# Seed tables of an S4D convolution: the second halves of five of eight sets made inside the attention loop

## The chip, the cores and the metric

The kernel runs on one core of a Trainium2 chip. The metric is device time in microseconds (us) of one execution. The core has five engines with an instruction queue each: TensorE (PE; its weight loads are listed as PEld), VectorE (DVE), ScalarE (ACT), GpSimd (POOL) and SyncE (SP), which issues all of this kernel's DMAs. Each engine takes its instructions in order, and waits on semaphores for the others.

## The reference

Two independent halves are computed and put side by side. Half A is a state-space convolution (S4D): a kernel K of 2048 taps for each of 448 channels is a sum over 256 complex modes, and it is convolved with the input u. Half B is attention with 16 heads of 28 channels over 2048 positions.

```python
dt = jnp.exp(log_dt)
A = -jnp.exp(log_A_real) + 1j * A_imag
C = (C_real + 1j * C_imag) * dt[:, None]
P = jnp.exp((A * dt[:, None])[:, :, None] * pos[None, None, :])
K = 2.0 * jnp.einsum("dn,dnl->dl", C, P).real
...
y = jnp.fft.irfft(Uf * Kf[None, :, :], L2)[:, :, :L]
y = y + u * D_skip[None, None, :]
...
qkv = (x @ wqkv).reshape(B, S, 3, H, Dh).transpose(2, 0, 3, 1, 4)
scores = jnp.einsum("bhqd,bhkd->bhqk", q, k) * scale
p = softmax(scores, axis=-1)
o = jnp.einsum("bhqk,bhkd->bhqd", p, v).transpose(0, 2, 1, 3).reshape(B, S, D) @ wo
return jnp.concatenate([a, b], axis=-1)
```

## The kernel before

The program has a prologue and a loop of 256 steps.

The prologue makes two things side by side. First, the projections of x to q, k and v, 48 of them, each of twelve matmuls; their results (`hl`, `vst`) are stored in DRAM. Second, the seeds. K is built in 56 blocks of 8 channels (`NB = 56`), and each block starts from a small table, its seeds: the first few powers of exp(A dt), C times such powers, and the factors for doubling. Seeds are made in eight sets (`NO = 8`) of seven blocks (`BO = 7`) by `seeds(o)`, which gives thirteen stages; set o begins four stages after set o - 1, and the 48 projections are spread over the first 37 stages (`PW = 37`). A set has a first half (load, exponent, scaling by dt, transposes on TensorE, phases, reduction, sines, sizes) which leaves the tile `tri` with cosine, sine and size of eleven powers (`LV = 11`). The second half multiplies these: `places`, `e_base`, `g_base`, `g_first`, `factors`, `g_copies` and two complex products on VectorE and GpSimd (`e3`, `e5`) fill the tiles `se` (named `qhat` in the profile, whose memory it borrows) and `sg`. `put_g` and `put_e` store them in `sd_d[o]`. Instructions of the prologue may be moved by the scheduler of the build.

At its end the prologue loads the first group's keys, q and v, and makes the row maxima of the first query unit (the max pass), 64 matmuls, each followed by a VectorE or ScalarE op.

The loop runs over 16 units (4 head groups x 4 chunks of 512 queries) of 16 key tiles each, so a group has 64 steps. Here every engine keeps the order of the program, which `ORDER` writes out for a step: four max matmuls (`m`, for the unit 16 + 3 steps ahead), four score matmuls (`s`) with an exponential on ScalarE each, the product with v (`pv`), two slots for other work (`f`), three places for VectorE (`v`), one place `k` for the kernel blocks. The other work:

- The kernel blocks of half A: `load_sd` brings a block's seeds, `e_power` (GpSimd, nine ops) and `g_powers` (VectorE) double them up to 64 and 32 powers, `k_mm` multiplies them on TensorE. A block may begin every `KP = 3.5` steps.
- The transform of u, in slots from step 3 to about 103.
- From step 192 (`12 * NK`) the spectra, and then the finish jobs, of half A, when the memory of the first keys is free; the second half of them, once the last kernel block is done.

Max matmuls, kernel blocks and all other work in the loop share three work banks of PSUM (`w_tile`). A group's keys fill the tile `khat` of 32 KB a partition; two such tiles (`k0_p`, `kq_p`) alternate between groups. `load_k` brings the next group's keys, one head at a time, at steps 17, 21, 25 and 29 of a group. The max matmuls of the next group begin at step 45 of a group.

Operands of VectorE inside the loop: `g_powers` works on `g` in SBUF and `zg` in PSUM, the maxima read PSUM, or PSUM and `rl` in SBUF.

Of the kernel before, what the change touches and what calls it, by code (L numbers as in the profile page):

```python
# [8 lines left out]
F32 = mybir.dt.float32  # L9
# [3 lines left out]
ALU = mybir.AluOpType  # L13
# [30 lines left out]
A0, A1, KW = 26, 34, (33, 35, 36)  # L44

# [45 lines left out]
def body(ctx, tc, a, out):  # L91
# [15 lines left out]
    sd_d = [dram.tile([BO, 128, SDF], F32, name=f"sd_{o}") for o in range(NO)]  # L107
    yu_d = dram.tile([128, N1, D], F32, name="yu_d")
# [102 lines left out]

    with ExitStack() as st:
# [97 lines left out]
        NH = BO * 16  # L310
        mul = lambda e, o_, x_, y_: e.tensor_tensor(o_, x_, y_, ALU.mult)

        def seeds(o):
# [5 lines left out]
            v = lambda t, k: t[:, k, :].rearrange("p (b h) -> p b h", h=16)  # L319
            vk = lambda t, k: t[:, k:k + 3, :].rearrange("p k (b h) -> p k b h", h=16)  # L320
# [8 lines left out]
            def turn():  # L329
                q["ps"] = ps = ps_n.tile([128, CQ], F32, name="pn")[:, :8 * PO].rearrange("p (a b h e) -> p a b h e", a=4, h=2, e=8)  # L330
                for i in range(4):
                    for h in range(2):
                        nc.tensor.transpose(ps[:, i, :, h, :], q["nat"][:, i, h * 128:(h + 1) * 128], ident[:PO, :PO])
                q["tr"] = s_p.tile([128, NH], F32, name="tr", bufs=2)
                act.activation(q["tr"], ps[:, 0].rearrange("p b h e -> p (b h e)"), AF.Copy)

            def phases():
                tri = t_p.tile([128, 3, LV, NH], F32, name="tri", bufs=2)
# [20 lines left out]
            def places():  # L359
                se = q_p.tile([128, HG, CQ], F32R, name="qhat", bufs=3).bitcast(F32).rearrange("p h q -> p (h q)")  # L360
                q["se"] = se = se[:, :BO * F_G].rearrange("p (b f) -> p b f", f=F_G)
                q["sg"] = sg = s_p.tile([128, BO, SDF - F_G], F32, name="sg", bufs=SGB)
                q["e8"] = se.rearrange("p b (c h e) -> p b c h e", c=2, e=8)
                q["g4"] = sg[:, :, :F_Z - F_G].rearrange("p b (c h e) -> p b c h e", c=2, e=4)
                q["zz"] = sg[:, :, F_Z - F_G:].rearrange("p b (k f h) -> p k b f h", k=6, f=3)
                pol.memset(q["e8"][:, :, 0, :, 0], 1.0)
                pol.memset(q["e8"][:, :, 1, :, 0], 0.0)

            def e_base():
                for k in range(3):  # L370
                    mul(pol, q["e8"][:, :, 0, :, 1 << k], v(q["mg"], k), v(q["r"], k))
                    mul(pol, q["e8"][:, :, 1, :, 1 << k], v(q["mg"], k), v(q["sn"], k))

            def g_base():

                q["gz"] = gz = s_p.tile([128, 2, 2, NH], F32, name="gz")
                mul(pol, q["r"][:, 6:8, :], q["mg"][:, 6:8, :], q["r"][:, 6:8, :])
                mul(pol, gz[:, :, 0], q["mg"][:, 6:8, :], q["sn"][:, 6:8, :])
                act.activation(gz[:, :, 1], gz[:, :, 0], AF.Copy, scale=-1.0)

            def g_first():

                c0 = q["ps"][:, 2:4].rearrange("p c b h e -> p c (b h e)")
                px = ps_x.tile([128, CQ], F32, name="px")
                c1, x_ = (px[:, i:i + 2 * NH].rearrange("p (c n) -> p c n", c=2) for i in (0, 2 * NH))
                g4_ = lambda e: q["sg"][:, :, :F_Z - F_G].rearrange("p b (c h e) -> p c b h e", c=2, e=4)[:, :, :, :, e]
                bh = lambda t: t.rearrange("p c (b h) -> p c b h", h=16)
                zr = lambda k: q["r"][:, 6 + k, :][:, None, :].to_broadcast([128, 2, NH])
                tt = vec.tensor_tensor
                for k, src, e, dst in ((0, c0, 1, bh(c1)), (1, c0, 2, g4_(2)), (1, c1, 3, g4_(3))):  # L390
                    tt(g4_(e), bh(src), bh(zr(k)), ALU.mult)
                    tt(x_, src[:, ::-1], q["gz"][:, k], ALU.mult)
                    tt(dst, g4_(e), bh(x_), ALU.add)
                q["c"] = c0, c1

            def g_copies():
                for c in range(2):
                    for e in range(2):
                        act.activation(q["g4"][:, :, c, :, e], q["c"][e][:, c].rearrange("p (b h) -> p b h", h=16), AF.Copy)

            def factors(i, k, p_, n_):
                zz, mg = q["zz"], q["mg"]
                mul(vec, zz[:, i:i + 3, :, 0, :], vk(mg, k), vk(q["r"], k))
                mul(vec, zz[:, i:i + 3, :, p_, :], vk(mg, k), vk(q["sn"], k))
                for k in range(i, i + 3):
                    act.activation(zz[:, k, :, n_, :], zz[:, k, :, p_, :], AF.Copy, scale=-1.0)

            def cmul(e, dst, s0, n, wr, wi, conj):

                if e is nc.vector:  # L410
                    x_ = ps_x.tile([128, CQ], F32, name="px")[:, :BO * 16 * n].rearrange("p (b h e) -> p b h e", h=16, e=n)
                else:
                    x_ = s_p.tile([128, BO, 16, 4], F32, name="x_e")[:, :, :, :n]
                br, bi = (w_[:, :, :, None].to_broadcast([128, BO, 16, n]) for w_ in (wr, wi))
                for c in range(2):
                    mul(e, dst[c], s0[c], br)
                    mul(e, x_, s0[1 - c], bi)
                    e.tensor_tensor(dst[c], dst[c], x_, ALU.add if (c == 0) == conj else ALU.subtract)

            sl = lambda t, i0, i1: [t[:, :, c, :, i0:i1] for c in range(2)]  # L420
            e8 = lambda *i: sl(q["e8"], *i)
            e3 = lambda: cmul(vec if o % 8 < E3 else pol, e8(3, 4), e8(1, 2), 1, q["e8"][:, :, 0, :, 2], q["e8"][:, :, 1, :, 2], False)
            e5 = lambda: cmul(pol, e8(5, 8), e8(1, 4), 3, q["e8"][:, :, 0, :, 4], q["e8"][:, :, 1, :, 4], False)
# [8 lines left out]
            fa, fb = lambda: factors(0, 3, 2, 1), lambda: factors(3, 8, 1, 2)  # L432
            return [[load], [exp_a] + dts(1, 2, 3), dts(0), [turn], [phases], [reduce], [sines], [sizes, g_base],
                    [places, fa, e_base], [e3, g_first], [fb, e5, g_copies], [put_g], [put_e]]
# [70 lines left out]
        n_stage = SP * (NO - 1) + len(stages[0])  # L505
# [110 lines left out]
    def load_sd(b):  # L616
        sds[b] = g_p.tile([128, SDF], F32, name="sdb", bufs=4)
        nc.sync.dma_start(sds[b], sd_d[b // BO][b % BO])
# [55 lines left out]

    def k_mm(b):
# [296 lines left out]
    def k_seed(s_):  # L972
        b = k_due[0] if k_due else NB
        if b < NB and b not in egs and done["mm"] >= b - 2 and K0 + b * KP <= s_ + (1 if b in es else 2):
# [31 lines left out]
    for s in range(NS):  # L1006
# [20 lines left out]
        if kt % 4 == 1 and u % NQ == 1 and u // NQ + 1 < G:  # L1027
            load_k(u // NQ + 1, kt // 4, k_pools[(u // NQ + 1) % 2])
# [4 lines left out]
        for op in ORDER:  # L1033
# [6 lines left out]
            elif op == "k":  # L1040
# [89 lines left out]
```

## Time and profile before

| what | value |
|---|---|
| median of 3 runs | 1301.34 us (1301.32 to 1303.18) |
| span of the profiled execution | 1301.1 us |
| mean granted TensorE clock | 0.978 |
| first score matmul of the loop | 254.0 us |
| last score matmul | 1275.7 us |
| busy: PE, DVE, ACT, POOL | 94%, 73%, 73%, 67% |
| HBM read, written | 120.73 MB, 82.18 MB |

The profile is of one execution. "Busy" is the union of an engine's instructions; matmuls are pipelined, so a busy TensorE need not be at its peak. A group of instructions is named by its engine, operation and tiles (out<-in). "A <-B" beside an idle time says that the engine sat idle until B was done. All lines of the kernel have the same line number in the profile, since a helper records every instruction; one goes by tiles. A timeline row gives start, duration, engine and instruction.

### The profile page before, as it was taken

What the parts mean: (1) busy time and instruction counts of PE and PEld (TensorE: products, weight loads), DVE (VectorE), ACT (ScalarE), POOL (GpSimd) and SP (SyncE); (2) the same over time, 40 slices, a digit from 0 to 9 for tenths busy, and PEclk for the clock granted to TensorE, in tenths of its full rate; (3) what the DMA queues carried; (4) which work ended last, traced back from release to release, by engine and by line L of the source; (5) the groups of instructions that cost most, each with busy time, mean ns of one, the idle gap of its engine ahead of it and who ended that gap; (6) DMA issues with size and microseconds to landing.
All of it is one profiled execution on the core that took longest, in us unless ns stands there. A gap on an engine that the chain in (4) does not pass through costs nothing.

```text
span 1301.1 us, 33177 instructions
## 1 busy us (share of the span) xinstructions
PE 1228.2 (94%) x12625; PEld 701.0 (54%) x12625; DVE 948.0 (73%) x2106; ACT 952.4 (73%) x2068; POOL 871.1 (67%) x736
## 2 busy tenths in 40 slices
PE   6878985899999999999999999999999999999997
PEld 5657763355555555555555555555555555544433
DVE  5887896987777887787788888888888655645111
ACT  4775763488888888888888888888887766756552
POOL 3676683298888878888869999998996212424421
PEclk9888997999999999999999999999999999999999
DMA  6677769835866555458644131733425453647656
GB/s 194 203 258 244 249 206 294 237 77 124 195 137 149 124 146 148 140 147 231 181 126 96 54 95 32 182 91 83 103 51 148 153 158 133 201 144 244 198 162 174
DMA packets 200088, 205.35 MB, mean 158 GB/s; under 512 B 95993, under 2 KB 158521, under 8 KB 197881
## 3 DMA queue, kind: packets, MB, share of 16 engines
q1 hardware_dynamic: 199928, 203.23, 56.2%
q8 instruction: 100, 1.64, 0.5%
q14 instruction: 60, 0.48, 0.1%
HBM read 120.73 MB, written 82.18 MB: 156 GB/s over the span
## 4 chain that ended last, share of the span: by engine, by line
PE 71%; DVE 10%; DMA 6%; POOL 5%; ACT 3%; issue 3%; SPq 0%; POOLq 0%; ACTq 0%; DVEq 0%
PE pm L75 40%; PE pss L75 16%; PE po L75 15%; DVE tri L75 2%; DVE mx L75 2%; POOL e L75 1%; POOL qhat L75 1%; DMA k<-hl 1%; ACT tri L75 1%; DVE qhat L75 1%; DVE sg L75 1%; DMA tri<-in_B_wqkv 1%; DVE px L75 1%; DMA khat<-k 1%; DMA ut<-in_A_u 1%
## 5 line engine op out<-in xcount | busy, mean ns | idle before, releaser
L75 ACT ACTIVATE p<-pss 128x512 f32<-128x512 f32 x1024 | 560.9, 609 | 111.6 <-PE pss L75 108.6
L75 PE MATMUL pss<-qhat,khat 128*128 128x512 f32 x1024 | 402.5, 399 | 1.5 <-ACT p L75 1.4
L75 DVE TENSOR_REDUCE mx<-pm 128x1 f32<-128x512 f32 x500 | 321.4, 684 | 109.2 <-PE pm L75 107.1
L75 PE MATMUL pm<-khat,qhat 128*128 128x512 f32 x749 | 326.3, 438 | 3.4 <-DVE mx L75 2.1
L75 POOL TENSOR_TENSOR e<-e,sdb 128x256 f32<-128x256 f32 x168 | 202.0, 1202 | 116.2 <-ACT e L75 61.2
L75 PE MATMUL po<-p,v 128*32 128x512 f32 x2048 | 269.1, 594 | 0.0
L75 POOL TENSOR_TENSOR e<-e,eu 128x256 f32<-128x256 f32 x168 | 248.4, 1478 | 13.2
L75 PEld LDWEIGHTS pm<-khat,qhat 128*128 128x128 f32 x749 | 141.0, 189 | 199.7 <-ACT p L75 47.8
L75 DVE CUSTOM_DVE_ANT_0 rl<-pm,rl 128x512 f32<-128x512 f32 x249 | 171.4, 688 | 65.2 <-ACT rl L75 61.5
L75 PEld LDWEIGHTS pss<-qhat,khat 128*128 128x128 f32 x1024 | 190.2, 188 | 45.7 <-issue 10.8
L75 POOL TENSOR_TENSOR eu<-e,sdb 128x256 f32<-128x256 f32 x168 | 202.2, 1203 | 0.0
L75 POOL TENSOR_TENSOR p<-pr,pr 64x448 f32<-64x448 f32 x64 | 73.3, 1145 | 158.5 <-PE pm L75 133.2
L75 ACT ACTIVATE rl<-pm 128x512 f32<-128x512 f32 x249 | 150.8, 606 | 20.4 <-PE pm L75 20.4
L75 DVE TENSOR_TENSOR g<-g,zg 128x128 f32<-128x128 f32 x392 | 162.1, 413 | 3.4
L75 PE MATMUL pm<-xh,khat 112*128 112x512 f32 x256 | 94.1, 451 | 23.2 <-DVE hl L75 11.1
L75 PE MATMUL pm<-kdif,qhat 128*128 128x512 f32 x249 | 100.5, 404 | 2.6 <-DMA v<-v 1.3
L75 DVE TENSOR_TENSOR zg<-g,zg 128x128 f32<-128x128 f32 x224 | 88.0, 393 | 5.0
L75 PEld LDWEIGHTS pm<-e,g 128*32 128x32 f32 x3584 | 57.2, 109 | 43.8 <-issue 16.1
L75 DVE TENSOR_TENSOR pr<-pm,ub 128x448 f32<-128x448 f32 x64 | 37.0, 619 | 56.4 <-PE pm L75 42.0
L75 PEld LDWEIGHTS pm<-xh,khat 112*128 112x128 f32 x256 | 54.2, 217 | 39.4 <-DVE hl L75 12.9
L75 PE MATMUL pm<-e,g 128*32 128x64 f32 x3584 | 73.0, 222 | 1.9 <-POOL e L75 1.9
L75 ACT ACTIVATE y<-pm 128x448 f32<-128x448 f32 x48 | 26.5, 553 | 58.2 <-PE pm L75 33.8
(134 smaller groups left out, 1470.3 us busy)
## 6 DMA issues: line engine op xcount, KB each, us to landing
sdb<-sd SPq DMA_DIRECT2D x56, 336.0 KB
khat<-k SPq DMA_DIRECT2D x64, 256.0 KB
qhat<-q SPq DMA_DIRECT2D x64, 256.0 KB
sd<-sg SPq DMA_DIRECT2D x8, 1456.0 KB
k<-hl SPq DMA_DIRECT2D x16, 512.0 KB
q<-hl SPq DMA_DIRECT2D x16, 512.0 KB
mw<-in_mw SPq DMA_DIRECT2D x16, 512.0 KB
sd<-qhat SPq DMA_DIRECT2D x8, 896.0 KB
```

The costliest lines, as they stand in the source:

```text
L75: i = f(*args, **kw)
```

## The change

Sets 0, 1 and 2 are made as before. For sets 3 to 7 (`LATE`) the prologue keeps the first half only. It then stores `tri` and a copy of C (`cp`) in a new DRAM tensor `tri_d[o]`, 15.7 KB a partition. The number of stages becomes 37.

In the loop `late_products(g)` takes the `khat` tile of the next group while that group's keys aren't yet due, and makes two sets in it in group 0, two in group 1 and one in group 2, 20 steps (`WIN`) each. One DMA at the first step of a window brings the powers and C; the ops of the second half are planned on steps 2 to 16; step 17 stores `sg` and `se` in `sd_d[o]`. `se` lies in the tile `og`, which grows to 7 KB. `planned(s, kind)` issues the DMAs at the start of a step, and the engines' ops after the `k` place of a step. The next group's keys are loaded at steps 40, 44, 48 and 52 of a group (`KL = 40`) in place of 17 to 29. Kernel blocks that begin in a window are 4 steps apart (`KW0`) in place of 3.5.

The products themselves are the same functions for early and late sets (`products`), in lists of single operations; in a late set C and the intermediate results `c1` and `x` lie in the `khat` tile in SBUF, where an early set has them in PSUM (`pn`, `px`).

```diff
+LATE, WIN, KW0, KL = ((3, 4), (5, 6), (7,)), 20, 4, 40
...
+    tri_d = [dram.tile([128, 3 * LV * BO * 16 + 2 * BO * 16], F32, name=f"tri_{o}") for o in range(NO)]
...
+    def products(q, temps, x_v, x_p, e_v=None):
...
+        ops["e"] = [lambda k=k, c=c: mul(pol, q["e8"][:, :, c, :, 1 << k], v("mg", k), v(("r", "sn")[c], k))
+                    for k in range(3) for c in range(2)]
...
+        for n, i, k, p_, n_ in (("fa", 0, 3, 2, 1), ("fb", 3, 8, 1, 2)):
+            ops[n] = [lambda i=i, k=k: mul(vec, q["zz"][:, i:i + 3, :, 0, :], vk("mg", k), vk("r", k)),
+                      lambda i=i, k=k, p_=p_: mul(vec, q["zz"][:, i:i + 3, :, p_, :], vk("mg", k), vk("sn", k))]
...
+        def first(k, src, e, last):
+            zr = lambda: q["r"][:, 6 + k, :][:, None, :].to_broadcast([128, 2, NH])
+            g4 = lambda e=e: q["g4"][:, :, :, :, e]
+            return [lambda: vec.tensor_tensor(g4(), bh(q[src]), bh(zr()), ALU.mult),
+                    lambda: vec.tensor_tensor(q["x"], q[src][:, ::-1], q["gz"][:, k], ALU.mult),
+                    lambda: vec.tensor_tensor(bh(q["c1"]) if last is None else g4(last), g4(), bh(q["x"]), ALU.add)]
...
+        ops["e3"] = cmul(vec, x_v, 3, 1, 1, 2)
+        ops["e5"] = cmul(pol, x_p, 5, 1, 3, 4)
...
+            def keep_c():
+                c = s_p.tile([128, 2, NH], F32, name="cp", bufs=2)
+                act.activation(c, q["c0"], AF.Copy)
+                nc.sync.dma_start(tri_d[o][:, 3 * LV * NH:], c.rearrange("p c n -> p (c n)"))
...
+            put_tri = lambda: nc.sync.dma_start(tri_d[o][:, :3 * LV * NH], q["tri"].rearrange("p t k h -> p (t k h)"))
...
-            return [[load], [exp_a] + dts(1, 2, 3), dts(0), [turn], [phases], [reduce], [sines], [sizes, g_base],
-                    [places, fa, e_base], [e3, g_first], [fb, e5, g_copies], [put_g], [put_e]]
+            begin = [[load], [exp_a] + dts(1, 2, 3), dts(0)]
+            if o in sum(LATE, ()):
+                return begin + [[turn, keep_c], [phases], [reduce], [sines], [sizes], [put_tri]]
+            p_ = products(q, temps, x_v, x_p)
+            return begin + [[turn], [phases], [reduce], [sines], [sizes] + p_["g"] + p_["gz"],
+                            [room] + p_["ones"] + p_["fa"] + p_["fan"] + p_["e"], p_["e3"] + [sums] + p_["c"],
+                            p_["fb"] + p_["fbn"] + p_["e5"] + p_["cc"], [put_g], [put_e]]
...
-        n_stage = SP * (NO - 1) + len(stages[0])
+        n_stage = max(SP * o + len(st_) for o, st_ in enumerate(stages))
...
+    def late_products(g):
...
+        def room():
+            x["t"] = k_pools[(g + 1) % 2].tile([128, HG, L], F32R, name="khat").bitcast(F32).rearrange("p h l -> p (h l)")
...
+            def load():
+                t, c = part(3 * LV * NH), part(2 * NH)
+                nc.sync.dma_start(x["t"][:, :at[0]], tri_d[o])
...
+                se = kq_p.tile([128, BO * F_G], F32, name="og").rearrange("p (b f) -> p b f", f=F_G)
...
+            def put():
+                nc.sync.dma_start(sd_d[o][:, :, F_G:].rearrange("b p f -> p b f"), q["sg"])
+                nc.sync.dma_start(sd_d[o][:, :, :F_G].rearrange("b p f -> p b f"), q["se"])
+                put_at[o] = True
...
+            plan[s0].append(("d", load))
+            at_ = {"v": (p_["fa"] + p_["fb"] + p_["e3"] + p_["c"], (2, 2, 3, 4, 5, 6, 6, 7, 8, 9, 10, 10, 11, 12, 13, 14, 14, 15, 16)),
+                   "p": (p_["ones"] + p_["e"][:4] + p_["g"] + p_["e"][4:] + p_["e5"], (2, 2, 3, 3, 4, 4, 5, 6, 7, 8, 10, 11, 12, 13, 14, 15)),
+                   "a": (p_["fan"] + p_["gz"] + p_["fbn"] + p_["cc"], (4, 5, 6, 7, 7, 8, 9, 10, 11, 12, 13))}
...
+            plan[s0 + WIN - 3].append(("d", put))
+
+        plan[g * NQ * NK].append(("d", room))
+        for i, o in enumerate(LATE[g]):
+            one(o, g * NQ * NK + WIN * i)
...
+    slow = [s for g, o in enumerate(LATE) for s in range(g * NQ * NK, g * NQ * NK + WIN * len(o))]
+    k_at = [K0]
+    while len(k_at) <= NB:
+        k_at.append(k_at[-1] + (KW0 if int(k_at[-1]) in slow else KP))
...
-        og_u[u] = og = kq_p.tile([128, G - 1, CQ], F32, name="og")
+        og_u[u] = og = kq_p.tile([128, BO * F_G], F32, name="og")[:, :(G - 1) * CQ].rearrange("p (g q) -> p g q", q=CQ)
...
-        if not (k_due and K0 + k_due[0] * KP <= s_ and k_due[0] in egs and not powers["e"] and not powers["g"]):
+        if not (k_due and k_at[k_due[0]] <= s_ and k_due[0] in egs and not powers["e"] and not powers["g"]):
...
-        if kt % 4 == 1 and u % NQ == 1 and u // NQ + 1 < G:
-            load_k(u // NQ + 1, kt // 4, k_pools[(u // NQ + 1) % 2])
+        n = s % (NQ * NK) - KL
+        if n >= 0 and n % 4 == 0 and n < 16 and u // NQ + 1 < G:
+            load_k(u // NQ + 1, n // 4, k_pools[(u // NQ + 1) % 2])
+        planned(s, "d")
...
+                for kind in "vpa":
+                    planned(s, kind)
```

More of the change, by code (lines that the diff above doesn't have):

```diff
@@ L335, in turn @@
                 act.activation(q["tr"], ps[:, 0].rearrange("p b h e -> p (b h e)"), AF.Copy)
+                q["c0"] = ps[:, 2:4].rearrange("p c b h e -> p c (b h e)")
+            def keep_c():
+                c = s_p.tile([128, 2, NH], F32, name="cp", bufs=2)
+                act.activation(c, q["c0"], AF.Copy)
+                nc.sync.dma_start(tri_d[o][:, 3 * LV * NH:], c.rearrange("p c n -> p (c n)"))
             def phases():
-                tri = t_p.tile([128, 3, LV, NH], F32, name="tri", bufs=2)
+                q["tri"] = tri = t_p.tile([128, 3, LV, NH], F32, name="tri", bufs=2)
                 q["r"], q["sn"], q["mg"] = r, sn, mg = tri[:, 0], tri[:, 1], tri[:, 2]
@@ L357, in sizes @@
                 act.activation(q["mg"], q["mg"], AF.Exp)
-            def places():
+            def room():
                 se = q_p.tile([128, HG, CQ], F32R, name="qhat", bufs=3).bitcast(F32).rearrange("p h q -> p (h q)")
[L361 to L379, printed above, removed]
@@ L381, in g_first @@
-            def g_first():
-                c0 = q["ps"][:, 2:4].rearrange("p c b h e -> p c (b h e)")
-                px = ps_x.tile([128, CQ], F32, name="px")
[L385 to L423, printed above, removed]
+                places(q, se[:, :BO * F_G].rearrange("p (b f) -> p b f", f=F_G),
+                       s_p.tile([128, BO, SDF - F_G], F32, name="sg", bufs=SGB))
@@ new lines, in temps, with sums @@
+            def temps():
+                q["gz"] = s_p.tile([128, 2, 2, NH], F32, name="gz")
+            def sums():
+                px = ps_x.tile([128, CQ], F32, name="px")
+                q["c1"], q["x"] = (px[:, i:i + 2 * NH].rearrange("p (c n) -> p c n", c=2) for i in (0, 2 * NH))
+            x_v = lambda n: ps_x.tile([128, CQ], F32, name="px")[:, :BO * 16 * n].rearrange("p (b h e) -> p b h e", h=16, e=n)
+            x_p = lambda n: s_p.tile([128, BO, 16, 4], F32, name="x_e")[:, :, :, :n]
@@ L616, in load_sd @@
     def load_sd(b):
+        assert b // BO not in sum(LATE, ()) or put_at[b // BO]
         sds[b] = g_p.tile([128, SDF], F32, name="sdb", bufs=4)
@@ L675, in k_mm, with planned @@
+    for g in range(len(LATE)):
+        late_products(g)
+    slow = [s for g, o in enumerate(LATE) for s in range(g * NQ * NK, g * NQ * NK + WIN * len(o))]
+    k_at = [K0]
+    while len(k_at) <= NB:
+        k_at.append(k_at[-1] + (KW0 if int(k_at[-1]) in slow else KP))
+    def planned(s_, kind):
+        for k, f in plan[s_]:
+            if k == kind:
+                f()
     def k_mm(b):
@@ L973, in k_seed @@
         b = k_due[0] if k_due else NB
-        if b < NB and b not in egs and done["mm"] >= b - 2 and K0 + b * KP <= s_ + (1 if b in es else 2):
+        if b < NB and b not in egs and done["mm"] >= b - 2 and k_at[b] <= s_ + (1 if b in es else 2):
             k_seeds(b)
     def k_begin(s_):
-        if not (k_due and K0 + k_due[0] * KP <= s_ and k_due[0] in egs and not powers["e"] and not powers["g"]):
+        if not (k_due and k_at[k_due[0]] <= s_ and k_due[0] in egs and not powers["e"] and not powers["g"]):
             return
```

60 lines of the change are left out of this document (55 added, 5 removed).

## The prediction

> **What bounds the kernel now.** I read the page first: the share of each engine in 40 slices of 32.5 us, and the chain of waits.
>
> ```profile
> span 1301.1 us, 33177 instructions
> ...
> PE   6878985899999999999999999999999999999997
> ...
> DVE  5887896987777887787788888888888655645111
> ACT  4775763488888888888888888888887766756552
> POOL 3676683298888878888869999998996212424421
> PEclk9888997999999999999999999999999999999999
> DMA  6677769835866555458644131733425453647656
> ...
> PE 71%; DVE 10%; DMA 6%; POOL 5%; ACT 3%; issue 3%; SPq 0%; POOLq 0%; ACTq 0%; DVEq 0%
> ```
>
> There are two regimes. In the first eight slices (the prologue) TensorE has gaps and its granted clock is 0.8 to 0.9, with no engine full. From slice nine on (the loop) TensorE is full, and the chain is 71% TensorE; the others run at eight or nine tenths, GpSimd highest. Next come stretches of my choice: busy us and instruction count of PE, PEld, DVE, ACT and POOL, then clock, DMA share and GB/s. Two rows for the score matmuls alone (PE, PEld, ACT) follow.
>
> ```profile
> 0.00:100.00 100.00, 75.32 (x313) 58.49 (x314) 75.65 (x139) 68.37 (x134) 58.40 (x74) 0.90 0.68 221
> 100.00:212.00 112.00, 89.69 (x394) 72.59 (x392) 89.46 (x152) 70.73 (x143) 76.54 (x85) 0.90 0.74 241
> 212.00:254.00 42.00, 32.27 (x78) 15.78 (x79) 34.82 (x78) 11.86 (x21) 0.81 (x2) 0.86 0.94 264
> 254.00:650.00 396.00, 394.43 (x4626) 215.39 (x4628) 311.53 (x738) 331.36 (x764) 331.23 (x260) 1.00 0.61 150
> 700.00:950.00 250.00, 249.16 (x3048) 142.74 (x3044) 218.35 (x522) 212.11 (x481) 234.72 (x186) 1.00 0.39 93
> ...
> 300.00:650.00 350.00, 137.57 (x348) 65.45 (x348) 190.32 (x347) 1.00 0.63 157
> 700.00:950.00 250.00, 110.79 (x280) 52.66 (x280) 153.14 (x281) 1.00 0.39 93
> ```
>
> Four score matmuls make a step, so a step takes 350 / 87 = 4.02 us while the transform of u also runs (steps 3 to about 103) and 250 / 70 = 3.57 us after it. VectorE is busy 79% and 87% there, GpSimd 84% and 94%. An op added to either in the loop meets an in-order queue with 0.84 / 0.66 us free in a u step and 0.45 / 0.22 us in a later one.
>
> **What leaves the prologue.** Per seed set the second half is 19 VectorE ops, 11 ScalarE ops and 16 GpSimd ops. All eight sets together, by tile (sg: DVE, ACT; gz: DVE, ACT, POOL; qhat: PE, PEld, DVE, POOL), and one GpSimd row more:
>
> ```profile
> 0.00:212.00 212.00, 45.64 (x80) 20.21 (x80) 0.90 0.71 232
> ...
> 0.00:212.00 212.00, 9.54 (x24) 3.11 (x8) 6.74 (x8) 0.90 0.71 232
> ...
> 0.00:212.00 212.00, 0.00 (x0) 0.00 (x0) 23.53 (x48) 86.76 (x112) 0.90 0.71 232
> ...
> L75 POOL TENSOR_TENSOR tri<-tri 128x224 f32<-128x224 f32 x8 | 7.3, 912 | 9.1 <-ACT tri L75 9.0
> ```
>
> VectorE: 78.7 / 8 = 9.8 us a set; GpSimd: 100.8 / 8 = 12.6; ScalarE: 23.3 / 8 = 2.9. Five sets take 49, 63 and 15 us away, nearly all from 100 us on, against one ScalarE copy (about 0.4 us, by its like in the sg tile) and one more put a set. Here is the prologue's part of the chain of waits, its sum by line and the pieces before the max pass:
>
> ```profile
> by line: DVE tri L75 10.1%; PE pm L75 9.7%; POOL qhat L75 6.5%; DMA k<-hl 5.9%; issue 5.6%; ACT tri L75 4.9%; DVE qhat L75 4.7%; DVE sg L75 4.6%; DMA tri<-in_B_wqkv 4.0%; DVE px L75 3.9%; DMA khat<-k 3.7%; POOL tri L75 3.3%; DVE mx L75 3.1%
> ...
> 201.61 6.66 DMA q<-hl
> 208.33 12.53 DMA k<-hl
> 220.88 10.06 DMA khat<-k
> 230.95 7.58 DMA v<-v
> ...
> sd<-sg SPq DMA_DIRECT2D x8, 1456.0 KB
> ...
> sd<-qhat SPq DMA_DIRECT2D x8, 896.0 KB
> ```
>
> Upper bound: the pieces of second halves (POOL qhat, DVE qhat, sg, px: 19.7% of the first 270 us, 53 us) leave for five of eight sets, 33 us. Lower bound: the stretch 201 to 238 waits on DMAs alone, and only set 7's put (2.35 MB at the 264 GB/s of 212 to 254) leaves it: 9 us. Between them: from 100 to 212 TensorE is idle 22 us; with VectorE down from 89 to about 40 us and GpSimd to about 14, ScalarE (58) and DMA remain. DMA carries 0.74 x 112 + 0.94 x 42 = 122 us of work in 154; each late set stores 2.0 MB of powers and C in place of 2.35, some 7 us less in all. I take half to two thirds of TensorE's idle time and most of the tail, 20 us; DMA would then be 86% busy, so more is unlikely. **Prologue: -20 (-33 to -9).**
>
> **What arrives in the loop.** The same 46 ops a set, spread over 20 steps; windows lie at steps 0 to 40 and 64 to 104 (u steps) and 128 to 148 (later ones). One thing changes besides the place: the c operands lay in PSUM (pn, px) and now lie in SBUF, so all 19 VectorE ops read two SBUF tensors, while today's VectorE ops in the loop read at most one. The seed rows give min/median/max ns, then two rows of the timeline:
>
> ```profile
> L75 DVE TENSOR_TENSOR sg<-tri x32: 490/510/1171, 39.1 to 196.7; 128x336 f32<-128x336 f32 x32
> L75 DVE TENSOR_TENSOR sg<-pn,tri x16: 549/566/585, 51.9 to 206.9; 128x224 f32<-128x224 f32 x16
> ...
> L75 DVE TENSOR_TENSOR qhat<-qhat x16: 356/516/2353, 45.9 to 200.5; 128x112 f32<-128x112 f32 x16
> ...
> L75 POOL TENSOR_TENSOR qhat<-qhat x16: 1016/1024/3532, 48.6 to 203.5; 128x336 f32<-128x336 f32 x16
> ...
> 160.70 2.25 POOL L75 TENSOR_TENSOR tri<-tr,pw 128x1232 f32<-128x1232 f32 x1 [0.46 <-ACT tr L75]
> 160.90 2.35 DVE L75 TENSOR_TENSOR qhat<-qhat 128x112 f32<-128x112 f32 x1
> ```
>
> The op with one input in PSUM (sg<-pn,tri) never varies. Those with two in SBUF reach twice to six times their minimum, and the last two rows show why: VectorE's 0.36 us op lasts until GpSimd's 2.25 us op is over. GpSimd's own op was held as well, up to 3.5 times its length. GpSimd and VectorE in the loop:
>
> ```profile
> L75 POOL TENSOR_TENSOR e<-e,sdb 128x256 f32<-128x256 f32 x168 | 202.0, 1202 | 116.2 <-ACT e L75 61.2
> L75 POOL TENSOR_TENSOR e<-e,eu 128x256 f32<-128x256 f32 x168 | 248.4, 1478 | 13.2
> L75 POOL TENSOR_TENSOR eu<-e,sdb 128x256 f32<-128x256 f32 x168 | 202.2, 1203 | 0.0
> L75 DVE TENSOR_TENSOR g<-g,zg 128x128 f32<-128x128 f32 x392 | 162.1, 413 | 3.4
> L75 DVE TENSOR_TENSOR zg<-g,zg 128x128 f32<-128x128 f32 x224 | 88.0, 393 | 5.0
> ...
> L75 POOL TENSOR_TENSOR eu<-e,sdb x168: 617/1062/1922, 253.8 to 990.3; 128x256 f32<-128x256 f32 x56, 128x512 f32<-128x512 f32 x56, 128x1024 f32<-128x1024 f32 x56
> L75 POOL TENSOR_TENSOR e<-e,eu x168: 732/1303/2405, 254.5 to 992.3; 128x256 f32<-128x256 f32 x56, 128x512 f32<-128x512 f32 x56, 128x1024 f32<-128x1024 f32 x56
> ```
>
> A block of the kernel transform costs GpSimd 652.6 / 56 = 11.65 us and VectorE 250.1 / 56 = 4.47. From the three sizes, an op that comes at a random moment of GpSimd's busy time finds 0.79 us left (sum of squares over twice the sum), times 0.84 busy: 0.66 us, the upper price of a wait. Lower price: the excess that such ops have in the prologue, 23.53 / 48 = 0.49 us a piece in the qhat tile beside a minimum of 0.36, 0.13 us. I take 0.5, nearer the upper, since GpSimd is fuller here than there. A set then costs VectorE 8.5 us (9.8 less that excess on its ten two-input ops) plus 19 x 0.5 = 18 us, 0.91 us a step, and GpSimd 11 us (12.6 less what held it) plus about 7 in which VectorE's 8.5 us hold it, 0.92 a step. Blocks come every 4 steps in place of 3.5, which gives back 0.16 (VectorE) and 0.42 (GpSimd) a step. Sums a u step: VectorE 3.16 - 0.16 + 0.91 = 3.91, GpSimd 3.36 - 0.42 + 0.92 = 3.86, both beside 4.02: some 97%. TensorE stands behind VectorE through three work banks in PSUM, so I put 0.2 us of stall on each of 80 steps, 16 us (2 without the waits, 32 with 0.66). In the later window VectorE needs 3.91 and GpSimd about 3.9 beside 3.57: 0.4 us over for 20 steps, 8 us, and 4 for unevenness: 12 (0 to 18).
>
> A rule of the Trainium skill speaks against this change: SBUF — State Buffer, section "Who interferes with whom", says that a VectorE instruction with two SBUF inputs and a GpSimd one that reads SBUF exclude each other, the second to start blocking fully. The seed rows agree (0.36 us became 2.35). If every op met it at random, the upper price would hold.
>
> **The other edits.** *Loads:* a set's 2.0 MB come in one DMA issued at its first step and are used two steps later, 8.0 or 7.1 us; at 264 GB/s it takes 7.6. VectorE and GpSimd wait in order, and behind them the max reductions that free TensorE's banks: 4 us over five loads (0 to 15). *Keys* of the next group load 23 steps later, five steps (20 us) before their first max matmul, behind the set's puts in SP's queue; 1 MB a head every four steps: nothing, but a late put would stop TensorE directly. SP has 15 more issues in the loop, none long. ScalarE gains 11 short ops a set, 0.15 us a step beside some 0.65 free. *Blocks* end 12.5 steps later (25 spacings of 4); TensorE's work in them only moves. Behind the last score matmul three finish jobs stand as built, not two; the row for that stretch:
>
> ```profile
> 1275.00:1301.00 26.00, 19.74 (x270) 8.03 (x266) 3.96 (x10) 4.79 (x9) 4.18 (x2) 0.96 0.54 146
> ```
>
> Twelve finish tasks and four projections in place of eight and four, at some 2 us, partly overlapped and taken from the loop: +2 (0 to 7).
>
> Sum against the profiled 1301.1 (the median of the runs, 1301.34, is the same within what follows): 1301.1 - 20 + 16 + 12 + 4 + 2 = **1315**.
>
> **The rivals.** *Faster:* the waits fall into the 0.8 us a step in which VectorE is free anyway (it waits for TensorE then), so the loop pays 4, the loads 2, the end 2, and the prologue gives 22: 1287. For it: blocks at 4 steps hand GpSimd 0.42 us a step; against: the later window has no such room. *The prologue hardly shrinks:* the first halves stay (DVE tri is the longest line of its chain) and the DMA tail gives 9: 1301 - 9 + 34 = 1326. *A convoy:* ScalarE's sign copies wait for GpSimd's products planned one step earlier; a GpSimd late by more than 4 us stops ScalarE, and with it every exponential. It decides once GpSimd passes 100% in u steps (a wait of about 0.66): the loop's upper bounds of 32 and 18, and 15 for the loads, give 1301 - 20 + 50 + 15 = 1346. *Even:* gain and price cancel within 0.2% (2.6 us, about what a measurement here can tell from none).
>
> **Chances.** Forecast 0.39, prologue 0.12, convoy 0.10: slower 0.61. Faster 0.33, even 0.06. The forecast's own range is 1304 to 1326; 8 in 10 reach from the faster rival's better half to below the convoy: 1280 to 1341.
>
> **What would show it.** First score matmul near 234 us in place of 254. In steps 0 to 40, 64 to 104 and 128 to 148: score matmuls at over 4.1 us a step, VectorE and GpSimd over 90%, VectorE's late ops well over 0.5 us, GpSimd's e ops no longer at three fixed lengths. Steps at 4.0 there, or late ops at their minimum, would prove the loop's price wrong; a first score matmul later than 245 the prologue's.

## The result, and the profile after

| | before | after |
|---|---|---|
| median of 4 runs | 1302.25 us (1301.32 to 1303.18) | 1380.36 us (1374.49 to 1382.24) |
| span of the profiled execution | 1301.1 us | 1372.4 us |
| first score matmul | 254.0 us | 236.5 us |
| step 192 begins | 983.6 us | 1019.1 us |
| step 255 begins | 1273.2 us | 1334.0 us |

The ratio is 1.0583, with a 95% interval of 1.0556 to 1.061: slower, as forecast, but by about five times as much (+14 forecast, +71 in the profiled execution), and beyond both ranges, which ended at 1326 and 1341 us. The traces below account for the profiled execution, 71.3 us longer in span; it is the shortest of the four.

The page of after: the slices (here of 34.3 us each) and the chain's shares by engine.

```profile
span 1372.4 us, 33229 instructions
...
PE   7879968899999999898999988999998799999996
...
DVE  5885538897887879878878998888886646553221
...
POOL 3662101987778888777599988799985733234331
PEclk9989988999999999999999999999999999999998
...
PE 62%; DVE 19%; POOL 6%; DMA 4%; ACT 4%; issue 4%; SPq 1%; POOLq 0%; DVEq 0%; ACTq 0%
```

The prologue is one slice shorter, and GpSimd is nearly empty at its end. In the loop TensorE's row has eights where it had nines, among them slice 31, and a seven at slice 32 (1064 to 1098 us), long after the last late set. VectorE's share of the chain went from 10% to 19%.

The windows view of after: busy us and instruction count of PE, PEld, DVE, ACT and POOL, then clock, DMA share and GB/s. The first three rows are the prologue, the next three the stretches of late sets (steps 0 to 40, 64 to 104, 128 to 148), then steps 192 to 208, then step 240 to the end.

```profile
0.00:100.00 100.00, 77.63 (x333) 60.17 (x333) 73.11 (x136) 69.59 (x136) 55.79 (x68) 0.93 0.68 222
100.00:212.00 112.00, 92.95 (x407) 71.06 (x407) 56.53 (x91) 66.67 (x102) 14.67 (x10) 0.95 0.86 289
212.00:236.50 24.50, 19.82 (x45) 9.44 (x45) 21.29 (x49) 6.70 (x13) 1.10 (x2) 0.80 0.61 151
236.50:409.00 172.50, 160.05 (x1683) 83.77 (x1682) 147.38 (x319) 135.51 (x307) 142.02 (x126) 0.99 0.58 149
503.80:684.70 180.90, 164.59 (x1860) 86.93 (x1858) 153.50 (x321) 142.72 (x342) 133.97 (x122) 1.00 0.58 176
776.00:863.90 87.90, 76.97 (x866) 41.69 (x865) 79.48 (x166) 64.89 (x147) 70.14 (x62) 0.96 0.38 104
1019.10:1104.20 85.10, 72.21 (x898) 39.73 (x897) 56.90 (x135) 52.50 (x115) 57.92 (x48) 0.92 0.40 122
1257.70:1372.40 114.70, 95.62 (x1116) 39.53 (x1112) 23.84 (x52) 45.77 (x87) 35.35 (x26) 0.95 0.66 197
```

The same steps before:

```profile
254.00:412.20 158.20, 157.73 (x1796) 85.44 (x1794) 123.77 (x293) 131.59 (x293) 134.94 (x106) 1.00 0.62 139
755.30:827.40 72.10, 71.81 (x898) 41.55 (x897) 62.05 (x148) 61.14 (x139) 69.51 (x56) 1.00 0.40 90
983.60:1049.00 65.40, 64.61 (x722) 36.59 (x721) 46.34 (x101) 47.61 (x98) 27.12 (x23) 1.00 0.56 171
```

Between 100 and 212 us GpSimd's work fell from 77 to 15 us, as foreseen, and VectorE's from 89 to 57, where about 40 had been foreseen. In steps 0 to 40 TensorE is busy 93% in place of 100%, yet neither VectorE (85%) nor GpSimd (82%) is full: the loss is a matter of who waits when, not of a full engine. In steps 192 to 208, where no late set is left, GpSimd has 58 us of work in place of 27, and TensorE is busy 85%.

Where the 71.3 us lie, for this kernel and all that were tried, from the start of every fourth score matmul in the traces. Each figure is a difference from the profiled execution of before, in us: the first score matmul, stretches of steps, and the time behind the start of step 255.

```text
run             span   first  0-40 40-64 64-104 104-128 128-148 148-192 192-208 208-240 240-255  tail
after          1372.4  -17.5 +14.3  +0.5  +18.5   +4.9   +15.8    -1.0   +19.7    -1.6    +7.2  +10.5
e1_spacing     1335.0   +1.2  -2.3  +0.4   -2.3   +2.4    -1.0    -1.0   +20.5    -1.6    +7.3  +10.5
e2_no_products 1319.1  -18.4  -2.2  +0.5   -2.2   +4.6    -0.9    -1.0   +21.4    -1.7    +7.4  +10.4
e3_one_input   1338.5  -16.8  +6.4  +1.0   +1.8   +5.9    +2.6    -0.9   +21.1    -1.7    +7.2  +10.8
e4_kp35        1355.5  -16.8 +25.0  +0.1  +30.5   +0.2   +14.2    +1.5    +0.0    -0.1    -0.1   -0.0
e5_join_dve    1346.5   +0.7  -2.3  +0.4   -2.4   +2.9    -0.9    -1.0   +28.2    +4.7    +4.5  +10.8
e6_join_act    1315.7   -2.5  -1.7  +0.4   -2.1   +0.7    -0.9    -1.0    +5.0    +1.3    +5.1  +10.5
e7_all_gpsimd  1349.7  -16.9  +8.7  +0.6   +8.3   +4.3    +6.2    -0.5   +21.1    -1.6    +7.3  +11.2
e8_both        1304.5  -17.0  +9.7  +0.0   +5.9   +0.2    +2.7    +1.8    -0.0    -0.1    +0.2   -0.0
v1_one_set     1315.3   +1.4 +10.9  +0.2   +0.0   +0.2    +0.0    +1.1    -0.0    -0.0    -0.1   +0.6
v2_one_pool    1307.2   +1.1  +0.4  +0.1   +1.2   +0.1    -0.1    +1.1    +0.0    +0.0    +0.2   +2.2
v3_two_pool    1298.9   -5.4  +0.4  +0.1   +1.6   +0.1    -0.2    +1.0    +0.0    +0.1    +0.2   -0.0
```

The change's own row has three parts: the prologue gives 17.5, the three windows (0 to 40, 64 to 104, 128 to 148) take 48.6, and 40.2 goes in stretches without any late set, 35.8 of it from step 192 on.

Two details for the theories. First the tile view of `khat` and `og`, VectorE's late ops by input (min/median/max ns, first and last start):

```profile
L76 DVE TENSOR_TENSOR khat<-khat x65: 384/848/2533, 245.8 to 850.8; 128x224 f32<-128x224 f32 x45, 128x336 f32<-128x336 f32 x20
L76 DVE TENSOR_TENSOR khat<-og x10: 354/736/1926, 263.1 to 813.3; 128x112 f32<-128x112 f32 x10
L76 DVE TENSOR_TENSOR og<-og,khat x10: 376/554/2430, 263.6 to 816.1; 128x112 f32<-128x112 f32 x10
L76 DVE TENSOR_TENSOR og<-og x10: 368/728/1754, 258.9 to 809.7; 128x112 f32<-128x112 f32 x10
```

The 95 ops take 91.5 us in all, 0.96 us each. Next the timeline of after around one of them (start, duration, engine, instruction, idle time before and its releaser):

```profile
532.39 2.39 POOL L76 TENSOR_TENSOR e<-e,eu 128x1024 f32<-128x1024 f32 x1
...
533.11 1.93 DVE L76 TENSOR_TENSOR khat<-og 128x112 f32<-128x112 f32 x1
```

The VectorE op starts in the middle of GpSimd's and ends 0.26 us after it: 1.93 us for one whose minimum is 0.35. VectorE keeps its order, so what stands behind this op, the row maxima that free TensorE's banks among it, comes later. The waits view of steps 0 to 40, for after and then for before (total us, times, longest):

```profile
PEld pm L76 <- DVE mx L76: 25.7, 34, 3.6
...
PE pm L76 <- DVE mx L76: 12.4, 9, 3.1
```

```profile
PEld pm L75 <- DVE mx L75: 10.8, 29, 0.8
```

TensorE's longest wait for a maximum grew from 0.8 to 3.6 us.

### The profile page after: what moved, and what is told of

The parts are those of the page before. It is cut to its first block, busy times and chain, and to the rows that moved or that the text cites. A ratio compares the mean times of both kernels' runs of the same rounds, so it can differ in the third digit from the quotient of the medians.

```text
span 1372.4 us, 33229 instructions
## 1 busy us (share of the span) xinstructions
PE 1246.5 (91%) x12625; PEld 696.8 (51%) x12625; DVE 977.2 (71%) x2106; ACT 963.9 (70%) x2075; POOL 865.6 (63%) x736
## 4 chain that ended last, share of the span: by engine, by line
PE 62%; DVE 19%; POOL 6%; DMA 4%; ACT 4%; issue 4%; SPq 1%; POOLq 0%; DVEq 0%; ACTq 0%
PE pm L76 36%; PE po L76 13%; PE pss L76 12%; DVE mx L76 4%; DVE khat L76 4%; DVE rl L76 2%; POOL e L76 2%; POOL p L76 2%; DVE zg L76 1%; DVE g L76 1%; SPq L76 1%; DVE tri L76 1%; DMA khat<-k 1%; DMA qhat<-q 1%; ACT rl L76 1%
## 5 line engine op out<-in xcount | busy, mean ns | idle before, releaser
L76 PE MATMUL pm<-khat,qhat 128*128 128x512 f32 x749 | 332.2, 446 | 45.2 <-DVE mx L76 40.7
L76 PE MATMUL po<-p,v 128*32 128x512 f32 x2048 | 274.6, 604 | 0.0
L76 POOL TENSOR_TENSOR eu<-e,sdb 128x256 f32<-128x256 f32 x168 | 206.1, 1227 | 0.0
L76 PE MATMUL pm<-xh,khat 112*128 112x512 f32 x256 | 87.1, 421 | 15.3 <-DVE kb L76 9.9
L76 PEld LDWEIGHTS pm<-e,g 128*32 128x32 f32 x3584 | 59.3, 111 | 56.7 <-POOL e L76 18.2
L76 PEld LDWEIGHTS po<-p,v 128*32 128x32 f32 x2048 | 56.0, 111 | 27.8 <-issue 23.6
```

Source lines behind the costliest of these rows:

```text
L76: i = f(*args, **kw)
```

## The experiments

Theory: late VectorE ops, held while GpSimd reads SBUF, delay the maxima (the windows), and the wider spacing of the kernel blocks alone costs what is lost after step 192. Rivals: the loads, puts and later keys; GpSimd's extra work; the plain number of VectorE ops. Each experiment is one execution (v3_again is twelve); the kernel before lies between 1300.4 and 1307.4 us in 17 executions on one chip, so whole times that differ by 2 or 3 us can't be told apart.

**e1_spacing**: the kernel before, with nothing of the change but the spacing.

```diff
+SLOW, KW0 = [*range(40), *range(64, 104), *range(128, 148)], 4
...
+    k_at = [K0]
+    while len(k_at) <= NB:
+        k_at.append(k_at[-1] + (KW0 if int(k_at[-1]) in SLOW else KP))
...
-        if not (k_due and K0 + k_due[0] * KP <= s_ ...
+        if not (k_due and k_at[k_due[0]] <= s_ ...
```

> The kernel before, with nothing of the change but the wider spacing of kernel blocks (4 steps in place of 3.5 in the same 100 steps). Theory A (the late blocks cost: they meet the spectra on GpSimd in steps 192 to 208, and push a finish job behind the last score matmul): steps 192 to 208 some 20 us longer than before, the stretch from step 240 to the end some 15 us longer, the windows a little shorter (up to 7 us in all), about 1330 us. Rival B (what is late at the end is late because of the products in the loop): within 3 us of before, 1301.

Measured: 1337.12 us beside 1304.16 on the same chip. The windows gain 5.6 us, and from step 192 on 36.7 is lost, beside the 35.8 of after. This part is the spacing's alone.

**e2_no_products**: after, with loads, puts, late keys and spacing, and no late op between; the late sets' products are left out, and the puts store loaded powers in their place.

```diff
-            for kind, (ops, steps) in at_.items():
+            for kind, (ops, steps) in ():
```

> The changed kernel without the 46 products a late set: loads, puts, late keys and spacing stay; the puts store a part of the loaded powers, so the kernel K of the late blocks is not computed. Theory A (the windows' 48 us are the products', VectorE's above all): the three windows lie within 5 us of before in all, the end as in the changed kernel, about 1327 us. Rival B (the 10 MB of loads, 12 MB of puts and the later keys cost, and VectorE waits for them): the windows keep 25 us or more, 1350 or more.

Measured: 1320.86 us beside 1304.16. The windows are 5.3 us shorter than before, about e1's figure: transfers of 2 MB in and 2.35 MB out cost nothing there as transfers. Steps 104 to 128, where keys now load, have +4.6 beside e1's +2.4; with blocks 3.5 steps apart (e4, e8) they have +0.2. What an op loses by waiting for its load isn't in this run.

**e3_one_input**: after, with the late VectorE ops replaced by reductions of one input over the same elements, so that the products themselves are left out.

```diff
+    class Reduced:
...
+        def tensor_tensor(self, o_, x_, y_, op):
+            return nc.vector.tensor_reduce(o_, x_[..., None], axis=AX.X, op=ALU.add)
...
+                "p (b h e) -> p b h e", h=16, e=n), lambda n: q["xp"](n), Reduced())
```

> The changed kernel with each late VectorE product replaced by an instruction of the same output size that reads one SBUF tensor (a reduction over one element), so the products are left out and the output differs. Theory A (about half of VectorE's 91 us of late ops is waiting for GpSimd's reads, and it costs about half of the windows' 48 us): late ops near 0.5 us with little spread, windows +20 to +28, about 1345 us. Rival C (only the number and length of the ops in VectorE's queue count, not the waits): windows still +45, within 5 us of 1372. Rival D (the waits are all): windows +5, about 1328.

Measured: 1340.46 us beside 1304.16. The tile view of e3 for `khat` and `og`:

```profile
L76 DVE TENSOR_REDUCE khat<-khat x65: 330/498/606, 247.2 to 815.7; 128x224 f32<-128x224 f32 x45, 128x336 f32<-128x336 f32 x20
L76 DVE TENSOR_REDUCE khat<-og x10: 347/360/377, 264.5 to 785.9; 128x112 f32<-128x112 f32 x10
...
L76 DVE TENSOR_REDUCE og<-og x20: 357/371/420, 260.2 to 788.2; 128x112 f32<-128x112 f32 x20
```

No op exceeds 0.61 us, with GpSimd as busy beside them as in after (83% of steps 0 to 40). The 95 take 43.5 us in place of 91.5, and the windows lose 10.8 us in place of 48.6, less than the 20 to 28 expected. So 48 us in which VectorE was held became 37.8 us of the kernel's time, and the ops' own length, with GpSimd's work and the waits for loads, makes 16 (10.8 against e1's -5.6). These ops differ from the late ones in the instruction too, not only in the number of inputs. But `g_powers` uses the late ops' instruction, TENSOR_TENSOR, with one operand in SBUF and one in PSUM, and in after, beside the same GpSimd, its 392 ops on `g` take 414 ns on average, where they took 413 before:

```profile
L76 DVE TENSOR_TENSOR g<-g,zg 128x128 f32<-128x128 f32 x392 | 162.4, 414 | 3.5
```

So what makes the difference is the second input in SBUF.

**e4_kp35**: after, with 3.5 steps in place of 4.

```diff
-LATE, WIN, KW0, KL = ((3, 4), (5, 6), (7,)), 20, 4, 40
+LATE, WIN, KW0, KL = ((3, 4), (5, 6), (7,)), 20, 3.5, 40
```

> The changed kernel with blocks 3.5 steps apart everywhere. Theory A: the last block ends as before, so steps 192 to 208 and the end lose most of their 37 us (down to 5 to 10), while GpSimd's and VectorE's windows, with 0.42 and 0.16 us a step more to do, cost 5 to 20 us more than the changed kernel's 48: about 1350 us. Rival E (GpSimd is the bound of the windows, and blocks slip anyway): windows +75 or more and the end late all the same, 1372 or above.

Measured: 1357.38 us beside 1304.16. Everything lost after step 192 is back (0.0), and the windows lose 69.7: the wider spacing had relieved them by 21, just above the 5 to 20 expected.

**e5_join_dve** and **e6_join_act** ask by which road the spacing costs time, both on e1. From step 192 the spectra join two products each with two GpSimd ops of 1.14 us (`p<-pr,pr`). e5 puts these on VectorE; e6 puts copies of one input on ScalarE in their place, which leaves the joins out.

```diff
-            nc.gpsimd.tensor_tensor(t_["p", e][:64], t_[0, 0][es], t_[1, 1][es], ALU.subtract)
-            nc.gpsimd.tensor_tensor(t_["p", e][64:], t_[0, 1][es], t_[1, 0][es], ALU.add)
+            nc.scalar.activation(t_["p", e][:64], t_[0, 0][es], AF.Copy)
+            nc.scalar.activation(t_["p", e][64:], t_[0, 1][es], AF.Copy)
```

> The kernel before with the 4-step spacing of e1, and the four products that join a spectrum (p<-pr,pr) on VectorE in place of GpSimd. Theory A (steps 192 to 208 lose 20 us because GpSimd, in order, makes 4.8 us of joins ahead of a late block's powers, for which TensorE stands in line): those steps come back to within 8 us of before, and the end by a few us less late than in e1: about 1322. Rival F (TensorE itself has more to do there, or the three PSUM banks are short): steps 192 to 208 stay at +16 to +21, 1333 to 1337.

> The kernel before with the 4-step spacing of e1, and the joins of a spectrum replaced by copies on ScalarE (the second product of each join is left out, so half A differs): GpSimd has no join at all, and VectorE no op that reads two SBUF tensors, which e5 had put there. Theory A (in steps 192 to 208 TensorE waits for block powers that stand behind 4.8 us of joins on GpSimd): those steps come back to within 8 us of before; the stretch from 240 to the end keeps most of its 18 us, since the spectra still lose slots to the blocks: about 1318 to 1325. Rival F (TensorE has more to do in those steps, or the PSUM banks are short): they stay at +16 to +21, 1333 to 1337.

e5 measured 1348.26 us beside 1303.09: worse than e1, and no test, since the joins then were two-input ops on VectorE beside the blocks' GpSimd ops. Its tile view of `pr` between 1000 and 1100 us:

```profile
L76 DVE TENSOR_TENSOR p<-pr,pr x12: 620/1402/2646, 1001.9 to 1062.7; 64x448 f32<-64x448 f32 x12
```

0.62 us at least and 1.40 in the median: they were stretched as the late ops were. e6 measured 1317.63 us beside 1303.9 (median of 17): steps 192 to 208 lose 5.0 us in place of 20.5. So the joins on GpSimd make 15.5 of the 20.5 us. The end (5.1 and 10.5) stays, so it has another cause.

**e7_all_gpsimd**: after, with VectorE's late products on GpSimd.

```diff
-        vec, pol, act = nc.vector, nc.gpsimd, nc.scalar
+        vec, pol, act = vec or nc.vector, nc.gpsimd, nc.scalar
...
-                "p (b h e) -> p b h e", h=16, e=n), lambda n: q["xp"](n))
+                "p (b h e) -> p b h e", h=16, e=n), lambda n: q["xp"](n), nc.gpsimd)
```

> The changed kernel with the late sets' 19 VectorE products on GpSimd. GpSimd gets 24 us a set, 58 of blocks and so 82 us in windows of 80 and 71. Theory A (what costs TensorE is VectorE held by GpSimd's reads, far more than GpSimd's own work): windows +10 to +20 in place of +49, the end as in the changed kernel: 1335 to 1345. Rival H (a full GpSimd costs as much, through the blocks' powers): windows +40 or more, 1365 or above.

Measured: 1351.61 us beside 1303.9. GpSimd's late work doubled (59.3 to 119.5 us), and the windows lose 23.2 us in place of 48.6, above the 10 to 20 expected. With twice the load on GpSimd the loss halved, so in after that load isn't what the windows mainly pay for; free it is not.

**e8_both**: e3 with the 3.5 steps of e4.

> e3 and e4 together: the five late sets' VectorE products replaced by one-input instructions of the same output size (the products are left out), and blocks 3.5 steps apart. Theory A (the change's loss is the held VectorE ops and the late blocks, and little else): the end costs nothing, the windows 12 to 28 us (e3's 11, and GpSimd with 0.42 us a step more), the prologue gives 17: 1297 to 1313. Rival I (3.5 steps fill GpSimd, and its lateness costs by itself what e4 paid over the changed kernel, 21 us or more above e3's 11): windows +32 or more, 1317 or above.

Measured: 1306.23 us beside 1304.78. With both losses away the change comes to nothing: the prologue's 17.0 us are paid back by 18.3 in the windows and 2 elsewhere. Against e4 the windows differ by 51.4 us, e3's finding again without the spacing: the 95 ops take 102.9 us in e4 and 43.6 here, so that 59 us of holding, 0.62 an op, became 51.4 us of the kernel's time.

**v1, v2, v3** look for a version that gains: fewer late sets, 40 steps each, 3.5 steps between blocks. v1 makes set 7 alone late, v2 does so with all products on GpSimd, v3 does that for sets 6 and 7.

```diff
-LATE, WIN, KW0, KL = ((3, 4), (5, 6), (7,)), 20, 4, 40
+LATE, WIN, KW0, KL = ((7,), (), ()), 40, 3.5, 40
...
-                    plan[s0 + i].append((kind, f))
+                    plan[s0 + 2 * i].append((kind, f))
```

> Set 7 alone is made late, in group 0, its ops spread over 40 steps, blocks 3.5 steps apart. The prologue has 37 stages here too. Theory A: the prologue gains 5 to 9 us (set 7's second half and its put stood at the end of it), the window costs 4 to 7 (19 waits of 0.45 us and 10 us of work, at half the density), the end nothing: 1297 to 1303. Rival G (a set costs the loop the same wherever it is spread, 14 to 17 us as with blocks 3.5 apart): 1308 to 1312.

> As v1, with the late set's 19 VectorE products on GpSimd, where no VectorE op meets its reads. GpSimd gets about 24 us in 40 steps, 0.6 us a step, to 3.33 of blocks: 3.93 of 4.02. Theory A (what costs is VectorE held by GpSimd): the window costs under 3 us, about 1296. Rival H (GpSimd that full comes late with the blocks' powers and TensorE waits): the window costs 8 us or more, 1302 or above.

> As v2 with sets 6 and 7 late, one in group 0 and one in group 1. The prologue gains 8 to 12 us. Theory A: the windows cost under 3 us each, about 1296. Rival H: 8 us or more each, 1308 or above.

> v3 (sets 6 and 7 late, one each in groups 0 and 1, all their products on GpSimd over 40 steps, blocks 3.5 steps apart), timed in rounds against the kernel before. By its one run (a first score matmul 5.4 us earlier, 3 us given back in the loop) it is 2 us faster, 0.998; if that run was luck, 0.9995 to 1.001.

Measured beside 1303.09 on one chip: v1 1317.27, v2 1308.94, v3 1300.71 us. In v1 19 ops over 40 steps, at 1.08 us each (20.6 in all), still cost those steps 10.9 us; on GpSimd 0.4. The window's price on GpSimd came out as expected (under 3 us a set), the prologue's gain did not: 5 to 9 us were expected of one late set and 8 to 12 of two, and the first score matmul moved by +1.4, +1.1 and -5.4. The end of the prologue still waits for DMAs, another set's puts first; in v1's chain of waits:

```profile
201.13 10.87 DMA sd<-sg
212.06 9.92 DMA sd<-qhat
222.00 12.51 DMA khat<-k
234.53 4.95 DMA v<-v
```

v3 again, in 12 runs, has 1303.84 us beside 1303.90 (17 runs), a ratio of 0.9995 (0.9982 to 1.0008): no difference. No version here beats the kernel before.

## Why the prediction was wrong

By its sum, 1301.1 - 20 + 16 + 12 + 4 + 2.

**Prologue, -20: right in size, in part by luck.** It measured -17.5, and from 106 us on no second half stands in the chain of after. But the sum took all of it from idle time of TensorE and the DMA tail. By the windows rows up to the first score matmul TensorE's busy time fell from 197.3 to 190.4 us for the same 785 instructions, at a granted clock of 0.95 in place of 0.90 between 100 and 212 us, and its idle time from 56.7 to 46.1: of the 17.5 us, 6.9 are shorter matmuls, a term that the sum didn't have. DMA was busy 0.82 of the time from 100 us to the first score matmul, where 0.86 had been worked out. (The prediction reads the clock of the prologue as 0.8 to 0.9; one slice there is at 7 tenths.)

**What a late op costs on VectorE: right.** 0.91 us a step was forecast, 18 us a set; 91.5 / 5 = 18.3 were measured. The wait is 0.51 us an op ((91.5 - 43.5) / 95, against e3), where 0.5 was taken between 0.13 and 0.66. The median against the minimum (0.85 and 0.38 us in the largest group), and e3, show the mechanism. The Trainium skill, "SBUF — State Buffer", section "Who interferes with whom", gives the same pair of instructions as mutually exclusive; e3's ops of one input (at most 0.61 us) and the unchanged ops on `g` bear it out.

**What it costs on GpSimd: too high.** About 7 us a set were added for GpSimd held by VectorE. Page rows of after:

```profile
L76 POOL TENSOR_TENSOR e<-e,sdb 128x256 f32<-128x256 f32 x168 | 203.1, 1209 | 174.4 <-ACT e L76 167.7
...
L76 POOL TENSOR_TENSOR e<-e,eu 128x256 f32<-128x256 f32 x168 | 248.4, 1479 | 13.2
...
L76 POOL TENSOR_TENSOR eu<-e,sdb 128x256 f32<-128x256 f32 x168 | 206.1, 1227 | 0.0
```

657.6 us in place of 652.6: 1 us a set. The late ops themselves take 11.9 a set, beside 11 forecast and 10.8 in e3. Of the signs named to look for, e ops away from their three lengths show in 29 of 504 only (over 5% above the median of their size, 5.6 us in all), GpSimd stayed at 82% and below, and VectorE at 85, 85 and 90% in the three windows. VectorE bears most of the waiting.

**"I put 0.2 us of stall on each of 80 steps": the first step that failed.** It measured (14.3 + 18.5) / 80 = 0.41 us. The reasoning added busy times, found 97% beside 4.02 us, and let most of the added 0.91 us fall into VectorE's free time. The sum of VectorE's work was nearly right: 3.68 and 3.84 us a step in the first two windows, where 3.91 was forecast. What failed is the conclusion that work which fits into 4.02 us costs little: the steps grew to 4.31 and 4.52 us, with VectorE 15% idle in them. Of the 48 us in which VectorE was held, 38 reached TensorE (e3). The waits view fits this: an op that lasts 1 to 2.5 us delays the maximum behind it then and there, and the free time lies elsewhere in the step. The later window, 12 forecast, measured 15.8, inside its bounds. The 4 us for the loads can't be read off by themselves: as transfers they cost nothing (e2), waits for them show once on VectorE (1.6 us) and once on GpSimd (5.3 us), and lie within the 16 us that e3 leaves. The windows as a whole were forecast at 32 and took 48.6.

**"Blocks end 12.5 steps later; TensorE's work in them only moves": the second, and the larger.** The sum had nothing for it but the +2 at the end; from step 192 on 35.8 us were lost. Two rows of the tile view of `e` and of `pr` on GpSimd, first in after, then in before (first and last start behind the comma):

```profile
L76 POOL TENSOR_TENSOR e<-e,eu x168: 717/1304/2492, 236.7 to 1108.9; 128x256 f32<-128x256 f32 x56, 128x512 f32<-128x512 f32 x56, 128x1024 f32<-128x1024 f32 x56
L76 POOL TENSOR_TENSOR p<-pr,pr x64: 1127/1144/1155, 1040.2 to 1319.0; 64x448 f32<-64x448 f32 x64
```

```profile
L75 POOL TENSOR_TENSOR p<-pr,pr x64: 1130/1144/1161, 1003.5 to 1247.8; 64x448 f32<-64x448 f32 x64
```

Before, the last block's op starts at 992.3 us (a row of the prediction) and the first join at 1003.5: they never meet. After, they meet from 1040 to 1109. The timeline of after there:

```profile
1065.68 4.81 POOL L76 TENSOR_TENSOR p<-pr,pr 64x448 f32<-64x448 f32 x4 [5.40 <-DVE pr L76]
1070.57 1.91 POOL L76 TENSOR_TENSOR e<-e,sdb 128x1024 f32<-128x1024 f32 x1
...
1074.42 2.32 POOL L76 TENSOR_TENSOR e<-e,eu 128x1024 f32<-128x1024 f32 x1
...
1076.80 1.08 PE L76 MATMUL pm<-e,g 128*32 128x64 f32 x32 [6.06 <-POOL e L76]
```

GpSimd waits 5.4 us for the joins' inputs, makes four joins, and only then the block's power; TensorE, next in order at that block's matmuls, stands for 6.06 us. With the joins away (e6) 15.5 of e1's 20.5 us go; where the other 5 come from stays open. The forecast had looked at the late blocks only as TensorE's work and in the tail, not at whom their GpSimd ops would meet.

**The end, +2 (0 to 7): too small.** From step 240 on it is 17.7 us, the same with the spacing alone (17.8), and nothing with 3.5 steps. From the start of step 255 on, the row of e1 and that of before, then the waits of e1 and those of before:

```profile
1297.00:1335.00 38.00, 24.48 (x316) 9.79 (x314) 6.45 (x18) 5.74 (x11) 7.04 (x4) 0.85 0.70 190
```

```profile
1273.00:1301.00 28.00, 21.45 (x278) 8.58 (x276) 3.96 (x10) 6.56 (x12) 4.18 (x2) 0.96 0.58 147
```

```profile
POOL ut L76 <- DMA ut<-in_A_u: 37.9, 4, 14.5
...
DVE ot L76 <- DMA og<-on: 8.9, 1, 8.9
...
PE pm L76 <- DMA zi<-z: 5.5, 1, 5.5
```

```profile
POOL ut L75 <- DMA ut<-in_A_u: 13.7, 2, 8.1
```

TensorE is busy 24.5 of 38 us in place of 21.5 of 28: more finish work than before stands there (316 instructions in place of 278, at a granted clock of 0.85 in place of 0.96), and TensorE waits 5.5 us for a load of `z`, where before it waited for one 0.3 us in all. That the finish jobs lost their slots in the loop to the late blocks is argued from this and from their first matmul (1236.4 us in after, 1162.3 before, 74 us later where step 208 begins 55 later); no run tried it by itself, so the cause of these 17.7 us within the spacing stays open.

**The rivals.** The faster one priced the loop at 4 us; even with one-input ops and 3.5 steps (e8) it is 18. The one whose prologue hardly shrinks had -9 there, and -17.5 was measured. The convoy, 1346, gave the loop 65 us by way of a GpSimd over 100%, which didn't occur (82% in steps 0 to 40). And no rival had a loss after step 192, which is 34 of the 57 us between the forecast's +14 and the measured +71; the windows are 17, the steps between the windows 4, the prologue 2.5.

## What to carry to other kernels

When work is put into the idle time of an in-order engine, ask what the longest single op will delay, not whether the sum fits: here, of 0.5 us of waiting per op behind GpSimd's long reads, about four fifths reached the engine that was the bound, with 15% of VectorE idle. When a paced producer is slowed, follow it to where its last items end, and look on every engine for the work that begins there. A prologue that ends in a chain of DMAs, as this one (v1), gives nothing back until the work that is taken out releases the last of them earlier.

## What was not expected of the hardware

- The waiting is one-sided. Against e3, the 95 VectorE ops take 48 us more; on GpSimd the 504 e ops and the 80 late ops take some 5 us more each (657.6 beside 652.5, 59.3 beside 54.0).
- The granted clock was 0.96 in steps 128 to 148 and 0.92 in steps 192 to 208, where before had 1.00. Gaps of TensorE alone don't tell when: in steps 64 to 104 it was busy 91% at a clock of 1.00. In steps 128 to 148 its busy time is 77.0 us in place of 71.8 although 32 matmuls fewer lie there (866 and 898), so at least 5 of that stretch's 15.8 us are longer matmuls, not waits.
